# Masks of the diagonal operands in a held PSUM bank, and the last diagonal operand made ahead of the iteration

## Chip, cores, metric

One core of one Trainium2 chip. The metric is device time in microseconds (us), the median of several executions of one kernel; lower is better. Engines are named as the profile names them: PE = TensorE (PEld its weight loads), DVE = VectorE, ACT = ScalarE, POOL = GpSimd, SP = SyncE, which issues the DMAs here. L68 and L74 in the profile's lines are helpers through which nearly all instructions are issued, so the lines are told apart by the names of their tiles.

## The reference, cut to what matters

Nystrom attention over 8 batches, 8 heads, 576 positions of 64, then a layer norm and a two-layer MLP with a residual:

```python
A = sm(q, k_lm); Bm = sm(q_lm, k_lm); C = sm(q_lm, k)       # 32 landmarks
Z = Bm.T / (norms of Bm)
for _ in range(6):
    Z = 2 * Z - Z @ Bm @ Z
x = A @ Z @ C @ v
out = x + relu(layernorm(x) @ w_ch1) @ w_ch2
```

## The kernel before

The six steps run on `st`, which holds 32 columns of an iterate and 64 columns that go with it. The heads of a unit lie below each other in the partitions, so a step multiplies with a block-diagonal operand `ebd`, which VectorE makes by multiplying `st`, repeated four times, with a mask. `bmbd` is the same thing for `Bm` and is needed once, after the sixth step. Batch 0 does without `ebd`; batch 1 goes through `attention`, batches 2 to 7 (the third to eighth) through `attention2`, in groups (2), (3, 4), (5, 6), (7). The MLP's products (`psh`, `pso`) are issued between the attention's, as filler.

```python
    maskw = const.tile([P, 4, 4], FP16, name="maskw")
    mask16 = const.tile([P, 4], FP16, name="mask16")           # both in SBUF
    ...
    ps1 = ctx.enter_context(tc.tile_pool(name="ps1", bufs=1, space=bass.MemoryType.PSUM))
    ...
    def diagonal(name, src, W, mask):
        t = asm.tile([P, W, 4, LM], FP16, name=name, tag=name, bufs=1)
        dve.tensor_tensor(out=t[:], in0=src[:, :, None, :].broadcast_to([P, W, 4, LM]),
                          in1=mask, op=ALU.mult)
        return t

    def masks(W):
        return mask16[:, None, :, None].broadcast_to([P, W, 4, LM])
    ...
    # attention2, after the products pscv = C @ v
        dve.reciprocal(out=rcv_, in_=pcv[:, :, :, D])
        dve.tensor_tensor(out=rcv[:], in0=rcv[:], in1=cinv[:], op=ALU.mult)
    ...
        for it in range(6):
            psn = p1([P, W, LM + D], "psn")                    # p1: the one buffer of ps1
            for w in range(W):
                MM(psn[:, w, lo:], ebd[:, w, :, :]..., st[:, w, lo:])
            ...                                                # st = 2 st - psn, VectorE
            if it < 5:
                ebd = diagonal("ebd", st[:, :, 0:LM], W, masks(W))
            else:
                bmbd = diagonal("bmbd", bm16, W, maskw[:, 0:W, :, None].broadcast_to(...))
```

Meanwhile GpSimd prepares later batches: it casts q, k and v to fp16 (`nat`, `natv`), adds them up to landmarks (`asum`, `s`), and centres finished blocks for the MLP (`xn`). An `xn` is turned by a transposing DMA into `xnT`, which the `psh` products read.

The softmax here doesn't subtract the row's maximum and nothing guards it: scores larger than these inputs give would overflow.

Of the kernel before, what the change touches and what calls it, by code (L numbers as in the profile page):

```python
# [9 lines left out]
FP16 = mybir.dt.float16  # L10
FP32 = mybir.dt.float32
# [5 lines left out]
P = 128  # L17
# [3 lines left out]
def kernel(  # L21
# [10 lines left out]
    nc = tc.nc  # L32
# [6 lines left out]
    LM = 32  # L39
# [12 lines left out]
        name=nc.get_next_instruction_name(), act_func_set_id=6, ins=[], outs=[]))  # L52

    const = ctx.enter_context(tc.tile_pool(name="const", bufs=1))
# [15 lines left out]
    dve, pool, scalar = Ordered(nc.vector), Ordered(nc.gpsimd), Ordered(nc.scalar)  # L70
    act = scalar.activation

    def MM(o, l, r, rb=0, cb=0, start=True, stop=True, skip=False):
        keep(nc.tensor.matmul(o, l, r, start=start, stop=stop, tile_position=(rb, cb),  # L74
                              skip_group_check=(skip or cb != 0)))
# [78 lines left out]
    mask4 = const.tile([P, 4], FP32, name="mask4")  # L154
# [16 lines left out]


    maskw = const.tile([P, 4, 4], FP16, name="maskw")
    mask16 = const.tile([P, 4], FP16, name="mask16")
    nc.gpsimd.tensor_copy(out=mask16[:], in_=mask4[:])
    for w in range(4):
        nc.gpsimd.tensor_copy(out=maskw[:, w, :], in_=(mask4t if w % 2 else mask4)[:])

# [99 lines left out]
    mout = ctx.enter_context(tc.tile_pool(name="mout", bufs=4))  # L278

    ps1 = ctx.enter_context(tc.tile_pool(name="ps1", bufs=1, space=bass.MemoryType.PSUM))  # L280
    ps2 = ctx.enter_context(tc.tile_pool(name="ps2", bufs=2, space=bass.MemoryType.PSUM))
    psM = ctx.enter_context(tc.tile_pool(name="psM", bufs=3, space=bass.MemoryType.PSUM))


    def warm(n, cols):
# [5 lines left out]
# [4 lines that stand above are left out]
        return t  # L295

    def masks(W):
        return mask16[:, None, :, None].broadcast_to([P, W, 4, LM])


    def attention(bs):
        units = [(b, u) for b in bs for u in range(U)]
        W = len(units)
        first = bs[0] == 0
        pool1, tag1 = (psM, "pm") if first else (ps1, "p1")

        def p1(shape, name):
            return pool1.tile(shape, FP32, name=name, tag=tag1)

        def p2(shape, dtype, name):  # L310
            return ps2.tile(shape, dtype, name=name, tag="p2")

        pss = p1([P, 2, W, 64], "pss")
        xT = {}
        for w, (b, u) in enumerate(units):
# [35 lines left out]
            out=qbd[:],  # L351
            in0=pss[:, 0, :, :].rearrange("p u (e l) -> p (u e) l", e=2)[:, :, None, :]
# [5 lines left out]


        psb = p1([P, W, LM], "psb")  # L360
        for w in range(W):
            for h in range(4):
# [8 lines left out]
        bm16 = asm.tile([P, W, LM], FP16, name="bm16", tag="bm16")  # L371
# [8 lines left out]
        for w in range(W):  # L380
# [8 lines left out]
            if w % 2 == 1:  # L389
                yield  # L390

        psse_ = p1([P, 4, W * LM], "psse")
        psse = psse_[:, 0:2, :].rearrange("p a (u l) -> p a u l", u=W)
        MM(psse[:, 0, :, :], bones[:].rearrange("p a c -> p (a c)"), bm16[:])
        for w in range(W):
            for h in range(4):
# [1 line left out]
                MM(psse[sl, 1, w, :], bmT[sl, w, :], bmT[sl, w, :], rb=32 * h, cb=32 * h)  # L398
        dve.tensor_reduce(out=psse_[:, 2, 0:W], in_=psse[:, 0, :, :], axis=AX.X,
                                op=ALU.max)  # L400
        dve.tensor_scalar(out=psse_[:, 3, 0:W], in0=psse_[:, 2, 0:W], scalar1=1e-6,
                                scalar2=None, op0=ALU.add)
        cinv = asm.tile([P, W], FP32, name="cinv", tag="cinv")
        dve.reciprocal(out=cinv[:], in_=psse_[:, 3, 0:W])
        st = asm.tile([P, W, LM + D], FP16, name="st", tag="st")
        dve.tensor_tensor(out=st[:, :, 0:LM], in0=psse[:, 1, :, :],
                                in1=cinv[:, :, None].broadcast_to([P, W, LM]),
# [1 line left out]
        if not first:  # L409
            ebd = diagonal("ebd", st[:, :, 0:LM], W, masks(W))  # L410
# [23 lines left out]
        for it in range(6):  # L434
# [16 lines left out]
            if not first and it < 5:  # L451
                ebd = diagonal("ebd", st[:, :, 0:LM], W, masks(W))
            if it < W:
                w = it
# [17 lines left out]
        for w, (b, u) in enumerate(units):  # L472
            z = zcbd_buf[w]
            dve.scalar_tensor_tensor(
                out=z[:, :, 0:D],
                in0=pszc[:, w, None, :].broadcast_to([P, 4, D]), scalar=cinv[:, w:w + 1],
# [127 lines left out]
    def scores(pair, lm, xT, of, sc, name):  # L604
        tiles = {w: ps2.tile([P, NJ, 2 * LM], FP32, name="ps" + name, tag="p2") for w in pair}
        for (j0, j1) in ((0, 8), (8, NJ)):
            for x in range(2):
                for w in pair:
                    for h in range(4):
                        rows = ds(32 * h, 32)  # L610
                        cb = 32 * ((h + 2 * (w % 2)) % 4)
                        MM(tiles[w][ds(cb, 32), j0:j1, :], lm[rows, w, :, x],
                           xT[of, w][rows, j0:j1, :, :, x], rb=32 * h, cb=cb,
                           start=(x == 0), stop=(x == 1), skip=True)
        res = []
        for w in pair:
            t = aexp.tile([P, NJ * 2 * LM], FP16, name=name, tag="e")
            act(t[:], tiles[w][:].rearrange("p c t -> p (c t)"), AF.Exp, scale=sc)
            res.append(t)
        return res  # L620

    def attention2(bs, c):
        units, lm, xT = c.units, c.lm, c.xT
        W = len(units)

        def p1(shape, name):
            return ps1.tile(shape, FP32, name=name, tag="p1")


        psb = p1([P, W, LM], "psb")  # L630
        ecT = {}
        for y in range(W // 2):
# [7 lines left out]
            if y == W // 2 - 1:  # L640
# [5 lines left out]
                bm16 = asm.tile([P, W, LM], FP16, name="bm16", tag="bm16")  # L646
# [9 lines left out]
                ecT[w] = t  # L656
            yield

        psse_ = p1([P, 4, W * LM], "psse")
        psse = psse_[:, 0:2, :].rearrange("p a (u l) -> p a u l", u=W)  # L660
        MM(psse[:, 0, :, :], bones[:].rearrange("p a c -> p (a c)"), bm16[:])
        for w in range(W):
            for h in range(4):
# [1 line left out]
                MM(psse[sl, 1, w, :], bmT[sl, w, :], bmT[sl, w, :], rb=32 * h, cb=32 * h)  # L665
        dve.tensor_reduce(out=psse_[:, 2, 0:W], in_=psse[:, 0, :, :], axis=AX.X,
                                op=ALU.max)
        dve.tensor_scalar(out=psse_[:, 3, 0:W], in0=psse_[:, 2, 0:W], scalar1=1e-6,
                                scalar2=None, op0=ALU.add)
        cinv = asm.tile([P, W], FP32, name="cinv", tag="cinv")  # L670
        dve.reciprocal(out=cinv[:], in_=psse_[:, 3, 0:W])
        st = asm.tile([P, W, LM + D], FP16, name="st", tag="st")
        dve.tensor_tensor(out=st[:, :, 0:LM], in0=psse[:, 1, :, :],
                                in1=cinv[:, :, None].broadcast_to([P, W, LM]),
                                op=ALU.mult)
        ebd = diagonal("ebd", st[:, :, 0:LM], W, masks(W))


        pscv = ps2.tile([P, 2, 512], FP32, name="pscv", tag="p2")
        for y in range(W // 2):  # L680
            for j in range(SEG):
                if j == NJ:
                    yield
                for x in range(2):
                    w = 2 * y + x
# [8 lines left out]
            if y + 1 < W // 2:  # L694
                yield
        v_used.update(c.bs)
        pcv = pscv[:, :, 0:(W // 2) * (D + 1)].rearrange("p x (y e) -> p y x e", e=D + 1)
        rcv = asm.tile([P, W], FP32, name="rcv", tag="rcv")
        rcv_ = rcv[:].rearrange("p (y x) -> p y x", x=2)
# [3 lines left out]
            out=st[:, :, LM:LM + D].rearrange("p (y x) e -> p y x e", x=2),  # L703
            in0=pcv[:, :, :, 0:D],
# [4 lines left out]
        for it in range(6):  # L709
            lo = 0 if it < 5 else LM  # L710
            psn = p1([P, W, LM + D], "psn")
            for w in range(W):
                MM(psn[:, w, lo:], ebd[:, w, :, :].rearrange("p a l -> p (a l)"), st[:, w, lo:])
            stn = asm.tile([P, W, LM + D], FP16, name="st", tag="st")
            dve.scalar_tensor_tensor(out=stn[:, :, lo:], in0=st[:, :, lo:], scalar=2.0,
                                           in1=psn[:, :, lo:], op0=ALU.mult,
                                           op1=ALU.subtract)
            st = stn
            if it < 5:
                ebd = diagonal("ebd", st[:, :, 0:LM], W, masks(W))  # L720
            else:
                bmbd = diagonal("bmbd", bm16, W,
                                maskw[:, 0:W, :, None].broadcast_to([P, W, 4, LM]))
            if it < W // 2:
                for e in scores((2 * it, 2 * it + 1), lm["k"], xT, "q", sc_A, "ea"):
                    ea.append(e)
            yield
# [5 lines left out]
        for w in range(W):  # L733
            z = zcbd_buf[2 + w]
            dve.tensor_tensor(
                out=z[:, :, 0:D],
                in0=pszc[:, w % 2, None, ds(D * (w // 2), D)].broadcast_to([P, 4, D]),
# [241 lines left out]


    a0, a1 = attention((0,)), attention((1,))

    def run(*who):
# [97 lines left out]
    for c, after, count in zip(sets, sets[1:] + [None], counts):  # L1081
        for step, _ in enumerate(attention2(c.bs, c)):
            work(count[step])
            if late and step >= 3:
                late.pop(0)()
            if after and after.done < len(after.parts) and not (
                    after.k_by_pool and after.spread(step)):
                next_cast()
            if after and step >= (5 if after.k_by_pool else 1):
                after.next_job()  # L1090
        while after and (after.jobs or after.lms):
            work(8)
            next_cast()
            after.next_job()
# [34 lines left out]
```

## Time and profile before

| | before |
|---|---|
| median of the first 3 runs | 328.93 us (327.85 to 329.19) |
| profiled run | 328.16 us, span 326.4 us |
| busy PE / DVE / ACT / POOL | 96 / 54 / 47 / 47% |

A busy share averages over stages with different limits. In this kernel TensorE, VectorE and GpSimd are busy in the first 140 us (131.6, 104.6 and 120.4 us of them), and in the rest TensorE alone is busy without a pause (182.2 of 186.4 us; VectorE 70.2, GpSimd 33.2). The prediction shows the lines.

Three lines from the timelines of the kernel before that the result will be held against: a cast of GpSimd near 49 us, an `xn` at 137.54 us, and the first MLP product behind the last wait for `xnT` (start us, duration us, engine, line, operation, tiles, shape, and in brackets the idle time before it).

```profile
49.49 1.15 POOL L68 CAST nat<-stg 128x1152 f16<-128x1152 f32 x1 [0.27 <-DVE ebd L68]
...
137.54 0.69 POOL L68 TENSOR_SCALAR xn<-xblk,mvg 128x512 f16<-128x512 f32 x1
...
140.54 1.89 PE L74 MATMUL psh<-xnT,w 128*128 128x512 f16 x8 [0.39 <-DMA xnT<-xn]
```

From the first of them to the end of the `xn` at 137.54 us GpSimd has no pause of over 0.1 us. These are 88.74 us (138.24 - 49.49, with unrounded times). The transposing DMA that the `psh` waits for was issued at 136.85 us, before that `xn` began, so it reads an earlier one. SyncE had issued it and the two transposes ahead of it with no pause of over 0.1 us from 132.98 us on, just after an `xn` that ended at 132.96 us. From 140.54 us to the end are 185.9 us in which TensorE does not pause until the last store.

### The profile page before, as it was taken

The page shows a single profiled execution, that of the slowest core. Times are in us where ns is not written, and L with a number is a line of the kernel's source. Part 1 is how long each engine was busy: PE and PEld are TensorE (multiplying, and loading weights), DVE is VectorE, ACT ScalarE, POOL GpSimd, SP SyncE. Part 2 cuts the span into 40 slices and gives each one's busy share as a digit, 9 for nine tenths or more (in the row PEclk, how much of TensorE's full clock was granted, in tenths as well). Part 3 has the DMA queues.
Part 4 walks back from the last instruction along what each step waited for, and adds up shares of the span by engine and source line. Part 5 has one row for each costly group of instructions (what it writes and reads, how often), then busy time and mean ns, then how long its engine had stood idle before and what let it go on. Part 6 is the DMA issues. An engine that isn't in the chain of part 4 may idle for free.

```text
span 326.4 us, 8246 instructions
## 1 busy us (share of the span) xinstructions
PE 313.8 (96%) x3406; PEld 162.0 (50%) x3406; DVE 174.8 (54%) x396; ACT 153.3 (47%) x308; POOL 153.6 (47%) x242
## 2 busy tenths in 40 slices
PE   8889989998999999999999999999999999999995
PEld 7537864553445444535544445454444444444444
DVE  3568769879965588864147668722566110010012
ACT  3646662848960572967204672454046107305600
POOL 3489888999999999999800044200013000000000
PEclk9999999999999999999999999999999999999998
DMA  7999999998699854598035013510251126032023
GB/s 278 391 355 363 382 401 297 330 324 254 215 220 234 242 150 139 142 246 152 2 80 87 2 27 69 98 34 2 64 128 2 32 64 98 0 73 60 0 47 81
DMA packets 36685, 50.34 MB, mean 154 GB/s; under 512 B 17828, under 2 KB 22696, under 8 KB 36648
## 3 DMA queue, kind: packets, MB, share of 16 engines
q1 hardware_dynamic: 36488, 49.69, 54.6%
q8 instruction: 26, 0.43, 0.6%
q10 hardware_dynamic: 160, 0.13, 0.2%
q14 instruction: 11, 0.09, 0.1%
HBM read 36.70 MB, written 9.44 MB: 141 GB/s over the span
## 4 chain that ended last, share of the span: by engine, by line
PE 59%; POOL 24%; DMA 8%; issue 3%; DVE 2%; ACT 1%; SPq 1%; POOLq 0%
PE psh L74 28%; PE pso L74 26%; POOL asum L68 13%; POOL nat L68 6%; DMA w1stg<-in_moe_w_ch_dram 4%; DMA stg<-in_v_dram 3%; POOL natv L68 2%; POOL xn L68 2%; PE psy L74 1%; PE pscv L74 1%; POOL s L68 1%; SPq L90 1%; DMA xnT<-xn 1%; ACT xn L68 1%; DVE ebd L68 1%
## 5 line engine op out<-in xcount | busy, mean ns | idle before, releaser
L74 PE MATMUL psh<-xnT,w 128*128 128x512 f16 (+1 forms) x640 | 134.0, 358 | 0.8 <-issue 0.5
L74 PE MATMUL pso<-w,hT 128*128 128x512 f16 (+1 forms) x592 | 132.9, 374 | 0.0
L68 ACT ACTIVATE hT<-psh 128x512 f16<-128x512 f32 x144 | 85.0, 597 | 97.3 <-PE psh L74 97.0
L74 PEld LDWEIGHTS <-w 128*128 128x128 f16 x640 | 59.5, 98 | 56.5 <-issue 3.4
L74 PEld LDWEIGHTS <-hT 128*128 128x128 f16 x592 | 56.0, 98 | 57.3 <-issue 0.8
L68 DVE SCALAR_TENSOR_TENSOR ot<-pso,rstd,xblk 128x512 f32<-128x512 f32 (+1 forms) x37 | 27.1, 733 | 78.1 <-PE pso L74 78.0
L68 POOL CAST nat<-stg 128x1152 f16<-128x1152 f32 x28 | 32.6, 1173 | 3.7 <-DMA stg<-in_q_dram 1.5
L68 POOL TENSOR_TENSOR asum<-asum 128x256 f32<-128x256 f32 (+2 forms) x54 | 28.3, 524 | 4.2
L68 DVE TENSOR_TENSOR xblk<-psy,rcpd 128x512 f32<-128x512 f32 (+1 forms) x40 | 27.6, 691 | 1.8 <-DVE rcpd L68 0.2
L68 POOL TENSOR_TENSOR asum<-nat 128x576 f32<-128x576 f16 x18 | 24.1, 1338 | 1.5
L68 DVE SCALAR_TENSOR_TENSOR st<-st,psn 128x192 f16<-128x192 f16 (+3 forms) x36 | 14.3, 396 | 19.3 <-PE psn L74 19.2
L68 POOL TENSOR_SCALAR xn<-xblk,mvg 128x512 f16<-128x512 f32 x14 | 9.6, 694 | 30.7 <-ACT junk L68 30.7
L68 POOL TENSOR_SCALAR negm<-mvg 128x1 f32<-128x1 f32 x14 | 2.7, 191 | 45.0 <-DVE mvg L68 40.4
L68 POOL CAST natv<-stg 128x1152 f16<-128x1152 f32 (+2 forms) x17 | 17.9, 1077 | 9.1 <-DMA stg<-in_v_dram 9.1
L68 DVE TENSOR_TENSOR ebd<-st,mask 128x256 f16<-128x256 f16 (+1 forms) x30 | 21.2, 707 | 1.0
L68 DVE STREAM_TRANSPOSE xT<-nat 128x576 uint32<-128x576 uint32 x24 | 18.2, 759 | 0.8 <-POOL nat L68 0.8
L74 PE MATMUL psy<-zcbd,ea 128*128 128x260 f16 (+1 forms) x80 | 15.9, 276 | 0.4
L68 ACT ACTIVATE ea<-psea 128x576 f16<-128x576 f32 x12 | 7.2, 648 | 16.6 <-PE psea L74 16.6
L74 PE MATMUL idle<-zeros 128*128 128x128 f16 (+2 forms) x79 | 12.3, 295 | 1.1 <-DVE eps_ln L180 1.1
L74 PEld LDWEIGHTS <-ea 128*128 128x128 f16 (+1 forms) x80 | 7.3, 100 | 11.1 <-issue 3.4
L68 DVE BATCH_NORM_STATS2 st<-xblk 128x6 f32<-128x512 f32 x18 | 12.4, 689 | 0.5
L68 ACT ACTIVATE junk<-xblk 128x512 f16<-128x512 f32 x14 | 8.8, 625 | 8.0 <-DVE xblk L68 7.7
(115 smaller groups left out, 261.3 us busy)
## 6 DMA issues: line engine op xcount, KB each, us to landing
stg<-in_q_dram SPq DMA_DIRECT2D x16, 576.0 KB, 6.6
out_dram<-ot SPq DMA_DIRECT2D x70, 128.0 KB, 2.4
stg<-in_k_dram SPq DMA_DIRECT2D x15, 576.0 KB, 4.9
stg<-in_v_dram SPq DMA_DIRECT2D x9, 576.0 KB, 6.7
w1stg<-in_moe_w_ch_dram SPq DMA_DIRECT2D x16, 256.0 KB, 6.0
w2stg<-in_moe_w_ch_dram SPq DMA_DIRECT2D x16, 256.0 KB, 5.3
stg<-in_v_dram SPq DMA_DIRECT2D x14, 288.0 KB, 5.1
xnT<-xn SPq DMA_TRANSPOSE x28, 3.7
```

The costliest lines, as they stand in the source:

```text
L68: return lambda *args, **kw: keep(getattr(self.engine, op)(*args, **kw))
L74: keep(nc.tensor.matmul(o, l, r, start=start, stop=stop, tile_position=(rb, cb), skip_group_check=(skip or cb != 0)))
L90: keep(queue.dma_start(out=t[:, r, j, :], in_=rows[r][:, :, j, :].rearrange("r p j d -> p r j d")))
```

## The change

The intent: VectorE's product for a diagonal operand reads two tensors from SBUF, and in the kernel before such a product and GpSimd's work beside it are both slow (`ebd` up to 1487 ns in place of 692, GpSimd's first sum 1637 in place of 1275); with its mask in PSUM it reads only one. No PSUM buffer is added: the one of `ps1` becomes a bank that is held for good, with the masks in its last 16 columns and everything that used `ps1` in its first columns. `bmbd` is made ahead of the steps, where VectorE waited for `pscv` in three of four stages (2.9, 4.0 and 4.6 us in the kernel before). Cut to the core (the rest replaces `ps1.tile` by `bank_of`, and puts two scratch rows of `psse` into one, so that they fit below the masks):

```diff
-    mask16 = const.tile([P, 4], FP16, name="mask16")
-    nc.gpsimd.tensor_copy(out=mask16[:], in_=mask4[:])
+    bank = ps1.tile([P, 512], FP32, name="bank")
+    pmask = bank[:, 496:512].rearrange("p (w h) -> p w h", h=4)
+    nc.vector.tensor_copy(out=pmask, in_=maskw[:])
     def masks(W):
-        return mask16[:, None, :, None].broadcast_to([P, W, 4, LM])
+        return pmask[:, 0:1, :, None].broadcast_to([P, W, 4, LM])
 ...
         v_used.update(c.bs)
+        bmbd = diagonal("bmbd", bm16, W, pmask[:, 0:W, :, None].broadcast_to([P, W, 4, LM]))
         ...
             if it < 5:
                 ebd = diagonal("ebd", st[:, :, 0:LM], W, masks(W))
-            else:
-                bmbd = diagonal("bmbd", bm16, W,
-                                maskw[:, 0:W, :, None].broadcast_to([P, W, 4, LM]))
```

More of the change, by code (lines that the diff above doesn't have):

```diff
@@ L280, with bank_of @@
     ps1 = ctx.enter_context(tc.tile_pool(name="ps1", bufs=1, space=bass.MemoryType.PSUM))
+    bank = ps1.tile([P, 512], FP32, name="bank")
     ps2 = ctx.enter_context(tc.tile_pool(name="ps2", bufs=2, space=bass.MemoryType.PSUM))
     psM = ctx.enter_context(tc.tile_pool(name="psM", bufs=3, space=bass.MemoryType.PSUM))
+    pmask = bank[:, 496:512].rearrange("p (w h) -> p w h", h=4)
+    nc.vector.tensor_copy(out=pmask, in_=maskw[:])
+    def bank_of(shape, name):
+        n = 1
+        for d in shape[1:]:
+            n *= d
+        assert n <= 512 - 16
+        names = [f"a{i}" for i in range(len(shape) - 1)]
+        if len(names) == 1:
+            return bank[:, 0:n]
+        return bank[:, 0:n].rearrange(f"p ({' '.join(names)}) -> p {' '.join(names)}",
+                                      **{k: d for k, d in zip(names, shape[1:])})
     def warm(n, cols):
@@ L304, in attention @@
         first = bs[0] == 0
-        pool1, tag1 = (psM, "pm") if first else (ps1, "p1")
         def p1(shape, name):
-            return pool1.tile(shape, FP32, name=name, tag=tag1)
+            return psM.tile(shape, FP32, name=name, tag="pm") if first else bank_of(shape, name)
         def p2(shape, dtype, name):
@@ L390, in attention @@
                 yield
-        psse_ = p1([P, 4, W * LM], "psse")
+        psse_ = p1([P, 3, W * LM], "psse")
         psse = psse_[:, 0:2, :].rearrange("p a (u l) -> p a u l", u=W)
@@ L400, in attention @@
                                 op=ALU.max)
-        dve.tensor_scalar(out=psse_[:, 3, 0:W], in0=psse_[:, 2, 0:W], scalar1=1e-6,
+        dve.tensor_scalar(out=psse_[:, 2, W:2 * W], in0=psse_[:, 2, 0:W], scalar1=1e-6,
                                 scalar2=None, op0=ALU.add)
         cinv = asm.tile([P, W], FP32, name="cinv", tag="cinv")
-        dve.reciprocal(out=cinv[:], in_=psse_[:, 3, 0:W])
+        dve.reciprocal(out=cinv[:], in_=psse_[:, 2, W:2 * W])
         st = asm.tile([P, W, LM + D], FP16, name="st", tag="st")
@@ L624, in attention2 @@
         W = len(units)
-        def p1(shape, name):
-            return ps1.tile(shape, FP32, name=name, tag="p1")
+        p1 = bank_of
         psb = p1([P, W, LM], "psb")
@@ L657, in attention2 @@
             yield
-        psse_ = p1([P, 4, W * LM], "psse")
+        psse_ = p1([P, 3, W * LM], "psse")
         psse = psse_[:, 0:2, :].rearrange("p a (u l) -> p a u l", u=W)
@@ L667, in attention2 @@
                                 op=ALU.max)
-        dve.tensor_scalar(out=psse_[:, 3, 0:W], in0=psse_[:, 2, 0:W], scalar1=1e-6,
+        dve.tensor_scalar(out=psse_[:, 2, W:2 * W], in0=psse_[:, 2, 0:W], scalar1=1e-6,
                                 scalar2=None, op0=ALU.add)
         cinv = asm.tile([P, W], FP32, name="cinv", tag="cinv")
-        dve.reciprocal(out=cinv[:], in_=psse_[:, 3, 0:W])
+        dve.reciprocal(out=cinv[:], in_=psse_[:, 2, W:2 * W])
         st = asm.tile([P, W, LM + D], FP16, name="st", tag="st")
```

## The prediction

> **What bounds the kernel now.** I read the page first (busy shares, slices, chain), then the waits of TensorE, then its timeline around each wait, then the groups by form for VectorE and GpSimd in stretches with and without company.
>
> From the page, the busy shares and the slices:
>
> ```profile
> PE 313.8 (96%) x3406; PEld 162.0 (50%) x3406; DVE 174.8 (54%) x396; ACT 153.3 (47%) x308; POOL 153.6 (47%) x242
> PE   8889989998999999999999999999999999999995
> POOL 3489888999999999999800044200013000000000
> PE 59%; POOL 24%; DMA 8%; issue 3%; DVE 2%; ACT 1%; SPq 1%; POOLq 0%
> ```
>
> TensorE is busy 313.8 of 326.4 us, so all its idle time together is 12.6 us; no change to waits can give more. In the windows view it is idle nowhere from 160 us to the final store. What can be won lies before that. GpSimd is at 8 or 9 tenths up to slice 20 (163 us), and the chain puts 24% on it, between 49 and 137 us. So two engines run level until about 140 us; after that TensorE alone sets the end, and time won at 140 us reaches the end whole.
>
> TensorE's waits between 35 and 145 us:
>
> ```profile
> engine line waited for: us in total, times, longest us
> PE psn L74 <- DVE ebd L68: 2.1, 3, 0.9
> PE psh L74 <- issue: 0.5, 1, 0.5
> PE psn L74 <- DVE st L68: 0.4, 1, 0.4
> PE psh L74 <- DMA xnT<-xn: 0.4, 1, 0.4
> PE psec L74 <- DVE xblk L68: 0.4, 1, 0.4
> PE pscv L74 <- DVE ecT L68: 0.2, 1, 0.2
> ```
>
> Half of what is left to win there is one thing: the product of an iteration step waiting for ebd, the block-diagonal operand that VectorE makes from st and a mask. Why is ebd late? Groups by form, first from 160 to 240 us, where GpSimd is nearly idle, then the whole run; last TensorE's and VectorE's timelines at the worst place:
>
> ```profile
> L68 DVE TENSOR_TENSOR ebd<-st,mask 128x512 f16<-128x512 f16 x5 | 3.5, 692 | 0.2
> L68 DVE TENSOR_TENSOR ebd<-st,mask 128x256 f16<-128x256 f16 x6 | 2.5, 425 | 0.2
> ...
> L68 DVE TENSOR_TENSOR ebd<-st,mask 128x256 f16<-128x256 f16 x18 | 11.2, 624 | 0.6
> L68 DVE TENSOR_TENSOR ebd<-st,mask 128x512 f16<-128x512 f16 x12 | 10.0, 832 | 0.4
> ...
> 121.53 1.49 DVE L68 TENSOR_TENSOR ebd<-st,mask 128x512 f16<-128x512 f16 x1
> 123.07 0.29 PE L74 MATMUL psn<-st,ebd 128*128 128x64 f16 x4 [0.67 <-DVE ebd L68]
> ```
>
> The same operation takes 425 or 692 ns alone, but up to 1487 ns while GpSimd reads. GpSimd suffers too: its first sum of a tile, by form, from 141 to 153 us (no ebd there) and from 110 to 125 us (an ebd about every 2.5 us):
>
> ```profile
> L68 POOL TENSOR_TENSOR asum<-nat 128x576 f32<-128x576 f16 x3 | 3.8, 1275 | 0.2
> ...
> L68 POOL TENSOR_TENSOR asum<-nat 128x576 f32<-128x576 f16 x3 | 4.9, 1637 | 0.2
> ```
>
> [...]
>
> [...]
>
> [...] with one PSUM input the 256-element products zcbd take 411 ns, and the 512-element xblk<-psy,rcpd takes 691 ns. So I use 420 and 690 ns for the new ebd.
>
> [...] The mask now shares the bank of psn, psb and psse. The iteration is a strict ring (psn, st, ebd, next psn), so TensorE never writes the bank while ebd reads it; nothing in this trace tests it.
>
> **The change part by part.**
>
> 1. Order. TensorE has the same 3406 products in the same order, GpSimd one tiny mask copy fewer, VectorE one 16-element copy more at the start, ScalarE and the queues the same. The waits of psn on TensorE's own semaphore go, and no psn gains an other-engine wait that its ring did not have. The fixed bank thus costs nothing and by itself saves nothing I can see.
>
> 2. ebd with one SBUF input. VectorE: 30 ebd take 11.2 + 10.0 = 21.2 us; at quiet speed 18 x 0.424 + 12 x 0.692 = 15.9 us. So 5.3 us of VectorE time go, all before 124 us. On the path, gap by gap from TensorE's timeline:
>  - 41.8 us, 0.40 idle: the first ebd took 0.85, 0.42 over its floor, and delayed st behind it. Closed: 0.40.
>  - 48.1 us, 0.53 idle: ebd took 1.14, 0.72 over. Closed: 0.53. At 49.6 us, 0.10 idle behind an ebd of 0.70: closed.
>  - 77.6 us, 0.87 idle: the ebd in front took 1.08 (0.66 over), and the one before 1.05, which pushed back the 1.34 us reduction between them. Together 1.28 over: closed, 0.87.
>  - 123.1 us, 0.67 idle: ebd took 1.49, 0.80 over. Closed: 0.67.
>  Sum 2.57 us, call it 2.6.
>
> 3. GpSimd, which must come along or the gain turns into a wait for xnT. Over the run, groups against their quiet means: asum<-nat 24.1 - 18 x 1.275 = 1.15; asum of 256, 13.5 - 18 x 0.724 = 0.47; asum of 128, 8.9 - 18 x 0.455 = 0.71; casts to nat 32.6 - 28 x 1.142 = 0.62; and 0.56 of idle before two casts, put down to ebd. Together 3.5 us, nearly all before 137 us; I count 3.3. GpSimd has no idle time over 0.1 us from 49.5 to 137 us, so it moves forward by that. Its end is what releases xn, the transposing DMA and then the psh at 140.54 us (0.39 idle). If TensorE gains 2.6 and GpSimd 3.3, that gap closes too: up to 0.4 more.
>
> 4. bmbd ahead of the six steps. Before, bmbd (0.63 to 0.68 us) lies between the last st and pszc. But TensorE has filler there and shows no idle before pszc: it is worth nothing. At its new place, ahead of the reciprocal of pscv, VectorE waits for pscv in three of four stages (idle 12.1 us for four of those reciprocals over the run). At 69.7 us it does not, and 0.42 us more there pass psn's margin (70.49 to 70.88 us) by perhaps 0.1 us: -0.1.
>
> Sum: 2.6 + 0.3 - 0.1, less about 0.1 for new small waits = 2.7 us. From 328.93: 326.2 us, 0.8% faster.
>
> **Rivals.**
>
> A. GpSimd becomes the bound. If its slow stretches come from other things than ebd (VectorE's transposes run beside it too), it gains 1 us, and TensorE then waits for xnT at 140 us. For: the chain has GpSimd without a break from 60 to 137 us. Against: from 141 to 153 us there are none of these iterations and its forms are at their floors. It would make 327.9 us.
>
> B. The PSUM operand is slower than I take it[...]. [...]
>
> C. TensorE is throughput-bound even where it seems to wait: the gaps close, and the following products, now queued more densely, do not start earlier, or a new wait (xblk, a score's exponent on ScalarE) takes their place. Against: the timelines show fillers of 1.7 us that end before psn, so TensorE really runs dry. Would give 327.5 us.
>
> D. More than the named gaps: with 5.3 us off VectorE in its fullest stretch (8 tenths busy from 40 to 100 us), other waits (ecT 0.2, xblk 0.4) shrink. Limit: all idle of TensorE from 35 to 145 us, about 5 us; 325.3 us likely the most.
>
> **Range and chances.** The three times of before spread over 1.3 us, so a median carries some 0.5 us. B and small forms of C and A are more likely than D: 325.2 to 327.5 us. Over 2% would need 6.6 us, more than TensorE's idle time after the first 35 us: 0.02. Slower by 2% needs a collision or a wait that the order does not show: 0.01.
>
> **What would show each step.** ebd rows near 420 and 690 ns in every stretch, with or without GpSimd beside them (step 2[...]). TensorE's wait for ebd at or near zero. asum<-nat near 1275 ns between 110 and 125 us (step 3). The psh now at 140.54 us starting 2.5 to 3 us earlier, with the same length from there to the end. If TensorE's idle before that psh grows to over 1 us, rival A holds. If bmbd's move shows a new wait of psn near 70 us of over 0.3 us, step 4 is wrong. A time over 328 us would mean that the gaps were not on the path at all.

The sum came to 2.7 us: 2.6 for TensorE's gaps, 0.3 for the gap before `psh`, less 0.1 for `bmbd` and 0.1 for new waits. Cut, where marked, is what no trace of this case had shown: the reason given for why an `ebd` with one SBUF input keeps its quiet speed beside GpSimd, so that step 2 rests there on an assumption of mine; an argument that VectorE loses no speed by it; a sentence on two engines in one bank; and the figure of rival B with the gain worked out from it, so that B stands only as a doubt. The 420 and 690 ns rest on `zcbd` (411 ns) and `xblk` (691 ns), products with one PSUM input in the kernel before.

## The result

| | before | changed |
|---|---|---|
| median, 6 runs each | 329.06 us (327.85 to 331.2) | 325.48 us (324.74 to 325.64) |
| ratio, with 95% interval | | 0.9879 (0.9845 to 0.9912) |
| ratio on another chip, 11 and 5 runs | | 0.9894 (0.9876 to 0.9912) |
| profiled span | 326.4 us | 323.4 us |

A ratio is the mean time of one kernel's fast runs over that of the other's of the same rounds, so it is not quite the ratio of the medians. The gain is 1.1 to 1.2%, some 3.5 to 4 us, where I had said 2.7. The two profiled runs differ by 3.05 us (328.16 and 325.11).

The page of the changed kernel: busy shares, the slices of TensorE and GpSimd, and the chain.

```profile
PE 313.4 (97%) x3406; PEld 163.8 (51%) x3406; DVE 170.7 (53%) x397; ACT 152.7 (47%) x308; POOL 149.7 (46%) x241
PE   8889999899999999999999999999999999999995
POOL 3389879999999999999500044200023000000000
PE 61%; POOL 23%; issue 3%; ACT 1%; DMA 1%; DVE 1%; POOLq 0%
```

TensorE is as busy as before, VectorE has 4.1 us less, GpSimd 3.9 us less. GpSimd has not left the chain: it holds 23% of a shorter span.

The groups by form of the changed kernel (busy us, mean ns), `ebd` over the whole run, and GpSimd's first sum from 110 to 125 us:

```profile
L68 DVE TENSOR_TENSOR ebd<-st,bank 128x512 f16<-128x512 f16 x12 | 8.2, 687 | 0.4
L68 DVE TENSOR_TENSOR ebd<-st,bank 128x256 f16<-128x256 f16 x18 | 7.6, 420 | 0.6
...
L68 POOL TENSOR_TENSOR asum<-nat 128x576 f32<-128x576 f16 x4 | 5.1, 1280 | 0.3
```

Every `ebd` is at its quiet speed, 420 and 687 ns in the mean and 689 at most, with GpSimd beside it or not, and GpSimd's sum went from 1637 to 1280 ns.

TensorE's waits in the changed kernel from 35 to 145 us (`bank` stands for `psn` and all else that lies in the held bank):

```profile
engine line waited for: us in total, times, longest us
PE psec L74 <- DVE xblk L68: 0.8, 2, 0.4
PE psh L74 <- DMA xnT<-xn: 0.8, 1, 0.8
PE bank L74 <- DVE st L68: 0.5, 1, 0.5
PE bank L74 <- DVE qbd L68: 0.2, 1, 0.2
```

The wait for `ebd` is gone. The wait for `xnT`, which I expected to close, is twice as long: TensorE comes to it first, and what it waits for comes from GpSimd. The lines of the changed kernel's timelines that answer to the three of before:

```profile
49.75 1.15 POOL L68 CAST nat<-stg 128x1152 f16<-128x1152 f32 x1 [0.28 <-PE bank L74]
...
134.52 0.70 POOL L68 TENSOR_SCALAR xn<-xblk,mvg 128x512 f16<-128x512 f32 x1
...
137.48 1.89 PE L74 MATMUL psh<-xnT,w 128*128 128x512 f16 x8 [0.76 <-DMA xnT<-xn]
```

GpSimd starts its stretch 0.26 us later and ends it 3.02 us earlier: 85.47 us in place of 88.74. The `psh` starts 3.06 us earlier, and from there to the end are 185.9 us again.

Both kernels issue the same 3406 products in the same order, so they can be compared one by one. TensorE's lead over the kernel before was 1.29 us at 49.6 us (the gaps of batch 1 had closed), but **0.13 us** at 70.9 us: it had given the lead back, 0.55 us of it before `psec`, 0.64 us before the first step of batch 2. From there to 123 us it grew to 3.42 us, and the wait for `xnT` cut it to 3.06. So there were two hypotheses to tell apart: TensorE's own gaps add up to the gain (my prediction), or **theory G**: GpSimd's stretch sets the time, and what TensorE wins beyond it is waited away.

### The profile page after: what moved, and what is told of

Read it like the earlier page. It is cut to its first block, busy times and chain, and to the rows that moved or that the text cites. A ratio compares the mean times of both kernels' runs of the same rounds, so it can differ in the third digit from the quotient of the medians.

```text
span 323.4 us, 8246 instructions
## 1 busy us (share of the span) xinstructions
PE 313.4 (97%) x3406; PEld 163.8 (51%) x3406; DVE 170.7 (53%) x397; ACT 152.7 (47%) x308; POOL 149.7 (46%) x241
## 4 chain that ended last, share of the span: by engine, by line
PE 61%; POOL 23%; issue 3%; ACT 1%; DMA 1%; DVE 1%; POOLq 0%
PE psh L74 29%; PE pso L74 26%; POOL asum L68 12%; POOL nat L68 6%; POOL natv L68 2%; POOL xn L68 2%; PE pscv L74 1%; PE psy L74 1%; POOL s L68 1%; PE bank L74 1%; DMA xnT<-xn 1%; ACT xn L68 1%; PE psea L74 1%; PE psec L74 1%; ACT xT L68 0%
## 5 line engine op out<-in xcount | busy, mean ns | idle before, releaser
L68 POOL CAST nat<-stg 128x1152 f16<-128x1152 f32 x28 | 31.8, 1144 | 3.7 <-DMA stg<-in_k_dram 1.7
L68 POOL TENSOR_TENSOR asum<-asum 128x256 f32<-128x256 f32 (+2 forms) x54 | 27.0, 500 | 4.2
L68 POOL TENSOR_TENSOR asum<-nat 128x576 f32<-128x576 f16 x18 | 23.0, 1276 | 1.5
L68 DVE SCALAR_TENSOR_TENSOR st<-st,bank 128x192 f16<-128x192 f16 (+3 forms) x30 | 12.2, 408 | 15.8 <-PE bank L74 15.7
L68 DVE TENSOR_TENSOR ebd<-st,bank 128x256 f16<-128x256 f16 (+1 forms) x30 | 15.8, 527 | 1.0
L74 PE MATMUL idle<-zeros 128*128 128x128 f16 (+2 forms) x79 | 13.2, 318 | 1.1 <-DVE eps_ln L178 1.1
```

The source lines that it names most:

```text
L68: return lambda *args, **kw: keep(getattr(self.engine, op)(*args, **kw))
L74: keep(nc.tensor.matmul(o, l, r, start=start, stop=stop, tile_position=(rb, cb), skip_group_check=(skip or cb != 0)))
```

## Experiments

Sixteen runs, three of them repeats of an earlier kernel. All gave correct results, those with constants in a bank that TensorE also writes included; by the program's order TensorE does not write there while `ebd` reads, and what an overlap would do was not tested. "To before" is the ratio to the kernel before on the same chip.

**1. A control.** The kernel before once more.

> The kernel before, unchanged, as a control and as a second look at it. The profiled run of before took 328.16 us, but its six runs have a mean of 329.3 and go from 327.9 to 331.2, while the six of the change go from 324.7 to 325.6. Theory S (scatter): where VectorE and GpSimd collide differs from run to run, so before scatters by its nature; then the copy against before gives a ratio near 1.000, but its runs spread over 1.5 us or more again, and its profile shows other ebd durations over 1 us at other places than the first profile (there 1.14, 1.05, 1.08, 1.06, 1.49 us). Rival: the scatter was of that chip or session; then the copy's ten runs stay within 1 us and the collisions are where they were.

Measured: 0.9996 (0.9975 to 1.0016), its runs from 328.10 to 329.77 us. After 110 us the collisions were elsewhere: `ebd` of over 1 us at 112.4 and 117.9 us (1.59 and 1.52), where the first profile had 0.84 and 0.69, and none at 121.5 us. Before 101 us they lay where they had been, one at 74 us a little under 1 us now. So where two instructions meet differs by run in part. The sum differs less: GpSimd's stretch was 89.01 us. The scatter of 1.67 us is as the theory had it, but kernels with masks in PSUM scatter by 0.7 to 1.8 us too (below), so most of it has another source.

**2. The parts one by one.** Masks back in SBUF, with the rest of the change:

```diff
-        return pmask[:, 0:1, :, None].broadcast_to([P, W, 4, LM])
+        return maskw[:, 0:1, :, None].broadcast_to([P, W, 4, LM])
     (and bmbd's mask from maskw)
```

> The change with its masks read from SBUF again (held bank and early bmbd stay). Theory [...]: all of the gain is the mask's place, so this is as slow as before: ratio to before 0.997 to 1.003, ebd of 256 elements back to a mean near 620 ns with single ones over 1 us, TensorE's wait for ebd back near 2 us. Rival 1 (early bmbd is worth something) or rival 2 (the held bank saves waits): ratio 0.990 to 0.995.

Measured: 1.002 (1.0002 to 1.0038), `ebd` of 256 elements at a mean of 636 ns. The gain is gone.

`bmbd` late, masks in PSUM (`bmbd` moved back behind the sixth step):

> The change with bmbd in its old place, after the sixth step, masks in PSUM. Theory: the move of bmbd is worth nothing or costs 0.1 us, so the ratio to before is that of the whole change, 0.985 to 0.991, and the 0.48 us wait of psn for st near 70.7 us that the changed kernel shows is gone. Rival 1: the move carries 0.3% or more; ratio 0.991 or higher.

Measured: 0.9914 (0.9894 to 0.9934). Most of the gain without the early `bmbd`. The 0.48 us wait before the first step was there as well (at 72.0 us), so it does not come from `bmbd`'s move.

The held bank alone (masks in SBUF, `bmbd` late):

> The kernel before with the held bank alone: masks in SBUF, bmbd late. Theory: the bank's fixed place changes only which semaphore a product waits on, ratio 0.998 to 1.002. Rival 2 (TensorE's waits on its own semaphore, which the held bank removes, cost time at each of the 24 steps): ratio 0.993 to 0.997.

Measured: 1.000 (0.9982 to 1.0017). The bank by itself is worth nothing.

**3. Which batches carry it.** The change whole, again, with the next three on one chip:

> The changed kernel once more, on the chip of the next three. Known now: in every kernel so far the psh behind the last wait for xnT (140.54 us before, 137.48 us changed) starts 185.9 us before the end, and from the third cast to nat (49.5 to 51 us) to the end of the last xn of that group GpSimd takes 88.6 to 89.0 us with masks in SBUF and 85.5 us with masks in PSUM. Theory G (GpSimd sets the pace from there): this profile shows 85.5 us again, and the ratio to before is 0.987 to 0.990. What is over 3.3 us must then lie in when the third cast starts. Rival (TensorE's own waits for ebd are the gain, as I predicted): ratio near 0.992, for these were 2.6 us.

Measured: 0.9894 (0.9876 to 0.9912), median 325.22 us; stretch 85.43 us; `psh` to end 185.9 us.

> The change with bmbd in its old place, again, now beside the whole change. Theory G: GpSimd's stretch is 85.5 us with either place of bmbd, so the two differ by under 0.3 us. Rival (the early bmbd is worth the 0.6 us that lay between the two kernels' medians of different sessions): 0.5 to 0.8 us slower than the whole change, with a wait before pszc in the profile.

Measured: 0.9915 (0.9895 to 0.9934), median 325.85 us, 0.6 us slower than the whole change, as before. The stretch is 85.45 us, the same. So not theory G's "under 0.3 us"; more under 7.

Masks in PSUM for batch 1 alone, or for batches 2 to 7 alone:

```diff
 a1_psum: attention2's ebd and bmbd
-                ebd = diagonal("ebd", st[:, :, 0:LM], W, masks(W))
+                ebd = diagonal("ebd", st[:, :, 0:LM], W, masks_sbuf(W))
 a2_psum: the same in attention
```

> The change with masks in PSUM in the stage of the second batch alone (its six ebd from 40 to 49 us); batches 3 to 8 read theirs from SBUF. My predicted sum (TensorE's gaps add up): 0.40 + 0.53 + 0.10 = 1.0 us faster than before, ratio 0.997. Theory G: TensorE's lead at 50 us is given back by 71 us to waits that hang on GpSimd, so only what moves the third cast counts: 0 to 0.5 us faster, ratio 0.9985 to 1.001; GpSimd's stretch stays near 88.8 us.

Measured: **1.0012** (0.9994 to 1.0031).

> The complement: masks in PSUM for batches 3 to 8, in SBUF for the second batch's stage. My predicted sum: 0.87 + 0.67 + 0.3 = 1.8 us faster than before, ratio 0.9945. Theory G: GpSimd's stretch 85.5 us, so 3.3 us faster, ratio 0.9895 to 0.9905, whatever TensorE waits for at 48 us.

Measured: **0.9906** (0.9890 to 0.9922).

These two decide against my sum. TensorE's waits (same stretch of time as above), first of a1_psum, then of a2_psum, and a2_psum's timeline around the `psh`:

```profile
PE bank L74 <- DVE ebd L68: 1.9, 3, 0.9
PE psh L74 <- DMA xnT<-xn: 0.9, 1, 0.9
...
PE bank L74 <- DVE st L68: 0.7, 2, 0.4
PE bank L74 <- DVE ebd L68: 0.6, 1, 0.6
...
137.72 0.38 PE L74 MATMUL pso<-w,hT 128*128 128x512 f16 x1
137.93 1.24 PE L74 MATMUL psh<-xnT,w 128*128 128x512 f16 x5
```

In a1_psum the three gaps of batch 1 that I had counted as 1.03 us are closed, and the kernel is no faster. In a2_psum they are all open (0.43, 0.56 and 0.11 us at 42 to 50 us in its trace), and it has nearly the whole gain. The stretch is 88.97 us in a1_psum and 85.44 us in a2_psum. But a2_psum is no plain case of theory G: its list has no wait for `xnT`, and the last transposing DMA landed at 137.04 us, 0.9 us before the `psh`. There TensorE came last, and its own lead, 2.61 us at the `psh`, is the gain of the profile.

**4. The collision without the late `ebd`.** `bmbd_late`, with one more product behind each `ebd` of batches 2 to 7, which nobody reads:

```diff
                 ebd = diagonal("ebd", st[:, :, 0:LM], W, masks(W))
+                diagonal("bmbd", st[:, :, 0:LM], W, maskw[:, 0:1, :, None]...)   # dup_sbuf; pmask in dup_psum
```

> bmbd_late (masks in PSUM, ratio to before 0.9915) with one more product of the same size behind each ebd of batches 3 to 8, whose result nobody reads (it goes to bmbd's buffer, which is rewritten before its use), its mask in SBUF. ebd itself is on time. Theory G: [...] GpSimd's stretch goes from 85.5 back to 88 to 89.5 us and the ratio to before is 0.999 to 1.005, though ebd stays at 420 and 690 ns. Rival (a late ebd is the cost): ratio 0.991 to 0.994, the price of VectorE's extra work alone.

Measured: 1.0019 (1.0001 to 1.0036), stretch 88.46 us.

> Control for dup_sbuf: the same extra product, its mask in PSUM. Theory G: GpSimd's stretch stays at 85.5 us; VectorE has some 7 us more to do before 125 us, so a few waits of TensorE grow; ratio to before 0.991 to 0.996, at least 1.5 us faster than dup_sbuf. Rival: no difference between the two.

Measured: 0.9991 (0.9975 to 1.0007), stretch 87.20 us, of which GpSimd idled 1.73 us before two `xn`, behind ScalarE. **My expectation failed.** The extra VectorE work alone costs 2.5 us (0.9991 against 0.9915 for bmbd_late). That it pushes back the step's own `st`, so that TensorE comes later and GpSimd waits for TensorE's rows, is my reading; of it, only GpSimd's idle time is shown. The pair differs by 0.3% and not by the 0.5% or more that I had asked for. In both profiles TensorE comes to the `psh` (141.80 and 140.53 us) without a wait. So against bmbd_late the added work costs 2.5 us with its mask in PSUM and 3.4 us with its mask in SBUF. The pair does not tell which of the two the kernel before suffered from.

**5. The last two-SBUF-input operation.** In the changed kernel, `rcv<-rcv,cinv` has 4 or 2 elements and takes 161 ns where GpSimd is idle. VectorE's and GpSimd's timelines in the (3, 4) stage:

```profile
106.91 0.82 DVE L68 TENSOR_TENSOR rcv<-rcv,cinv 128x4 f32<-128x4 f32 x1
...
106.44 1.27 POOL L68 TENSOR_TENSOR asum<-nat 128x576 f32<-128x576 f16 x1
```

It ends at 107.73 us, 0.02 us after GpSimd's sum does (107.71 us). The product of 2 elements at 69.43 us took 0.94 us and ended at 70.37 us, a sum of GpSimd beside it at 70.34 us.

```diff
-        dve.reciprocal(out=rcv_, in_=pcv[:, :, :, D])
-        dve.tensor_tensor(out=rcv[:], in0=rcv[:], in1=cinv[:], op=ALU.mult)
+        inv = bank[:, 480:480 + W]
+        dve.reciprocal(out=inv.rearrange("p (y x) -> p y x", x=2), in_=pcv[:, :, :, D])
+        dve.tensor_tensor(out=rcv[:], in0=inv, in1=cinv[:], op=ALU.mult)
```

> The change, with its last two-SBUF-input VectorE operation mended too: rcv<-rcv,cinv of 4 or 2 elements takes 161 ns alone but 0.82 to 0.98 us in the two stages where GpSimd runs, and ends with the GpSimd instruction it waited for. The reciprocal now goes to four free columns of the held bank. rcv<-bank,cinv should take 160 to 230 ns everywhere, and the 0.48 us wait of TensorE for st near 71 us go. Theory G: GpSimd sets the time, so the gain over the whole change is 0 to 0.3 us (ratio to before 0.9885 to 0.9900). Rival (TensorE's wait adds up): 0.5 us or more, 0.9878.

Measured: 0.9891 (0.9875 to 0.9907). The tile's view, then TensorE's wait for `xnT`:

```profile
L68 DVE TENSOR_TENSOR rcv<-bank,cinv x4: 159/160/161, 69.6 to 216.1; 128x2 f32<-128x2 f32 x2, 128x4 f32<-128x4 f32 x2
...
PE psh L74 <- DMA xnT<-xn: 1.3, 1, 1.3
```

It took 160 ns everywhere, the 0.48 us wait at 71 us went, and the time stayed within the noise: the 0.5 us turned up again as a longer wait for `xnT` (1.33 us in place of 0.76). Stretch 85.49 us. This is theory G in small: a TensorE wait was removed, and in the profile nothing of it reached the end.

**6. GpSimd's time itself, longer and shorter.**

> The change, with two of the four casts of v for batches 4 and 5 made twice by GpSimd (2 x 1.15 = 2.3 us more, near 85 us; the same values are written). No other engine has more to do. Theory G: GpSimd's stretch 87.8 us and the time 2.3 us more less nothing, for GpSimd is already the last to come (TensorE waits 0.7 us for xnT): 327.5 us, ratio to before 0.996 to 0.998, TensorE's wait for xnT near 3 us. Rival (GpSimd's time only moves along): ratio unchanged at 0.989 to 0.990.

```diff
+                if self.bs == (3, 4) and w >= 2:
+                    pool.tensor_copy(out=natv_of[b][:, ds(SEG * u, SEG), 0:D], in_=stg[:])
                 pool.tensor_copy(out=natv_of[b][:, ds(SEG * u, SEG), 0:D], in_=stg[:])
```

Measured: **0.9983** (0.9970 to 0.9995), median 328.02 us. No other engine got work. The stretch is 88.06 us, 2.6 us longer than in the two profiles of the change, and the profiled time (327.94 us) is 2.2 to 2.8 us longer than theirs (325.76 and 325.11). TensorE's waits in it:

```profile
PE psy L74 <- DVE xblk L68: 1.3, 2, 1.1
PE psh L74 <- DMA xnT<-xn: 1.3, 1, 1.3
```

The wait for `xnT` is 1.3 us and not 3, but there is a new one of 1.3 us some 9 us before it, in the rows. So more time on GpSimd moves the end of the changed kernel back, about one for one.

For the other direction, casts of v go to ScalarE:

```diff
+                if self.bs == (3, 4) and w % 2 == 1:      # v_act_rcv; gp_minus1: w == 3; gp_minus2: also (5, 6), w == 0
+                    scalar.copy(natv_of[b][:, ds(SEG * u, SEG), 0:D], stg[:])
+                    return
```

> rcv_psum, and two of the four casts of v for batches 4 and 5 (1.15 us each on GpSimd, near 84 to 88 us) are given to ScalarE. Theory G: GpSimd's stretch falls to about 83.2 us, and the time falls until TensorE's own work is the bound: it waits 0.7 us for xnT now, plus the 0.5 us that rcv frees, so 0.7 to 1.3 us faster than the whole change, ratio to before 0.985 to 0.987. Rival (GpSimd is not the bound): no gain, or a loss of some tenths through ScalarE's longer queue.

> rcv_psum (ratio 0.9891, TensorE waits 1.3 us for xnT) with one cast of v for batch 5 on ScalarE, the one that had its data in v_act_rcv. Theory G: GpSimd's stretch 84.3 us, gain 0.8 to 1.15 us, ratio to before 0.9855 to 0.987, TensorE's wait for xnT down to 0.2 to 0.5 us. Rival: ratio stays 0.989.

> gp_minus1 and one cast of v for batch 6 on ScalarE, in its idle time near 121 to 126 us. GpSimd's stretch 83.2 us. Theory G with TensorE close behind: TensorE's wait for xnT goes and its own work becomes the bound, so 1.2 to 1.6 us faster than rcv_psum, ratio 0.984 to 0.986; not the whole 2.3 us. Rival: 0.989.

Measured: 1.0067 (1.0048 to 1.0086), 1.0119 (1.0099 to 1.0140) and 1.0131 (1.0113 to 1.0148). All three failed as tests, for one reason, seen in gp_minus1's ScalarE and TensorE timelines:

```profile
80.57 1.15 ACT L68 CAST natv<-stg 128x1152 f16<-128x1152 f32 x1 [5.37 <-DMA stg<-in_v_dram]
...
82.27 2.29 PE L74 MATMUL psh<-xnT,w 128*128 128x512 f16 x5 [5.91 <-ACT hT L68]
```

ScalarE reaches the cast before its load has landed and idles 5.37 us, and a product of TensorE waits 5.91 us for an `hT` that ScalarE makes after the cast. GpSimd comes to its casts of v later: in the changed kernel it makes these four from 83.76 us on and does not wait for a load there. In v_act_rcv the other cast stood in front and had taken the stall (4.45 us), which is why I thought that this one had its data. Whether less work on GpSimd would make the kernel faster stays untested.

**7. Does early `bmbd` work through `rcv`?** rcv_psum with `bmbd` late:

> rcv_psum with bmbd in its old place. If the early bmbd works by moving rcv<-rcv,cinv to where GpSimd blocks it for less long (1.27 and 0.86 to 1.09 us with bmbd late, 0.93 and 0.82 to 0.98 us with it early), then with rcv out of GpSimd's way the place of bmbd no longer matters: within 0.3 us of rcv_psum, ratio 0.988 to 0.990. If bmbd's own 0.4 to 0.7 us between the last st and the next product is what it saves, late_rcv is 0.5 to 0.7 us slower than rcv_psum: 0.991.

Measured: 0.9907 (0.9894 to 0.9921). By the numbers that is the second answer, but the profile does not bear it out: stretch 85.51 us and wait for `xnT` 1.33 us, both as in rcv_psum (85.49 and 1.33). The two profiles differ by 0.9 us in when the stretch begins.

What the traces of the decisive kernels show, in order of the stretch. "Begins" is the start of the third cast to `nat` after 40 us, where the stretch begins; it ends with the same `xn`, counted by its place in GpSimd's order (my expectations call this `xn` the last of its group; it is the next one). "`psh`" is the same product in all, number 1849 of TensorE's 3406. TensorE waits for `xnT` before it, 0.2 to 1.3 us, in all rows but two: in bmbd_late_again the wait is 0.04 us, in a2_psum there is none.

| kernel | masks, batches 2 to 7 | `bmbd` | begins | stretch | `psh` | span | to before |
|---|---|---|---|---|---|---|---|
| mask_sbuf | SBUF | early | 50.83 | 89.04 | 142.00 | 327.9 | 1.0020 |
| before_copy | SBUF | late | 49.62 | 89.01 | 140.74 | 326.6 | 0.9996 |
| a1_psum | SBUF | early | 50.35 | 88.97 | 141.48 | 327.4 | 1.0012 |
| before | SBUF | late | 49.49 | 88.74 | 140.54 | 326.4 | 1 |
| bank_only | SBUF | late | 50.16 | 88.64 | 141.00 | 326.9 | 1.0000 |
| gp_plus | PSUM, 2 casts more | early | 49.80 | 88.06 | 140.34 | 326.2 | 0.9983 |
| late_rcv | PSUM | late | 50.55 | 85.51 | 138.60 | 324.5 | 0.9907 |
| rcv_psum | PSUM | early | 49.66 | 85.49 | 137.68 | 323.6 | 0.9891 |
| changed | PSUM | early | 49.75 | 85.47 | 137.48 | 323.4 | 0.9879 |
| bmbd_late | PSUM | late | 50.97 | 85.46 | 138.49 | 324.4 | 0.9914 |
| bmbd_late_again | PSUM | late | 50.44 | 85.45 | 138.36 | 324.2 | 0.9915 |
| a2_psum | PSUM | early | 49.75 | 85.44 | 137.93 | 323.8 | 0.9906 |
| after_again | PSUM | early | 50.53 | 85.43 | 138.18 | 324.0 | 0.9894 |

In every row span less `psh` is 185.9 us. Begin plus stretch gives the end of GpSimd's part; `psh` follows 2.1 to 2.8 us later. The begin scatters by 1.5 us and goes with a load: in the six profiles that begin at 50.3 us or later, GpSimd had just waited 0.7 to 1.1 us for weights (`w2stg`), and in the six that begin by 49.8 us it had not. The two pauses between the three casts are 0.26 to 0.30 us in all, whatever the trace names as their end. The stretch does not scatter: 88.6 to 89.0 with masks in SBUF, 85.4 to 85.5 with masks in PSUM.

None of these is a version that clearly beats the change; rcv_psum equals it.

## Why the prediction was wrong

**The cause** of the gain was named right. It is the place of the masks: back in SBUF the whole gain is lost (mask_sbuf, 1.002, `ebd` of 256 elements at a mean of 636 ns), in PSUM `ebd` is at its quiet speed (689 ns at most, 1487 before), and the held bank costs and saves nothing (bank_only 1.000). Rival B, a slow PSUM operand, fell: 420 and 687 ns against 425 and 692. Of rival C the first half fell: the products behind the closed gaps did start earlier. Its second half, a new wait in their place, came true for batch 1, and for `xblk`, which it had named. Rival D's 325.3 us is nearly the time measured, but by luck: of the waits that it named, the one for `ecT` stayed at 0.15 us and the one for `xblk` grew from 0.39 to 0.77 us.

**The step that failed is the sum of step 2, "Sum 2.57 us, call it 2.6", and the place that step 3 gave GpSimd**, as one that "must come along". I had GpSimd's term right, 3.3 us in the prediction and 3.3 us in the stretches (88.74 - 85.47), and then used it only to ask whether one small gap would close. But before the change GpSimd was the later of the two: TensorE waits 0.2 to 1.0 us for `xnT` in all five profiles with these masks in SBUF. So what TensorE wins alone is given back (a1_psum), and the gain could be as large as GpSimd's 3.3 us, as far as TensorE kept up.

The sum was also too small for what it meant to add. I took a gap's idle time for its delay. The record of an MLP product, which stands before most of these gaps, lasts 0.38 us, and the next one starts 0.22 us after its start where nothing is waited for (five `pso` took 1.24 us together in the kernel before), so that up to 0.16 us of a delay lies hidden under the record before. Compared product by product, the five gaps were worth 0.43, 0.70, 0.26, 1.03 and 0.84 us of TensorE's lead: 3.26 us and not 2.57.

Term by term: batch 1's gaps (0.40, 0.53, 0.10 of idle time) are worth nothing while GpSimd is slow (a1_psum, 1.0012). TensorE closed them and gave the lead back by 71 us, to new waits before `psec` and before the first step. With GpSimd fast they may be worth some of it: a2_psum leaves them open, begins its stretch with the changed kernel at 49.75 us and is as long in it, but its `psh` starts 0.45 us later, without a wait. The medians on one chip were 325.67 and 325.22 us; the intervals overlap. The 0.87 and 0.67 us of the later batches are part of a lead that grew by 3.3 us between 71 and 123 us: 1.03 and 0.84 of it are these gaps, 0.62 lies before a `psh` at 110.4 us, where the trace puts the wait down to nothing, and five steps of 0.18 to 0.29 us, less three small losses, are the rest. The 0.3 us for the gap before `psh` had the wrong sign; that wait grew from 0.39 to 0.76 us.

**The base** was a second error of the range. I subtracted from the median, 328.93, what I had counted in a run that took 328.16. The profile's begin of the stretch, 49.49 us, is the earliest of all kernels in the table; an average run probably begins later. In the profiled pair the whole difference is 3.05 us, and the ratio of the first session (0.9879) has one high run of before in it, 331.2 us; on another chip it was 0.9894, or 3.5 us. What between 3.1 and 4 us is the stretch and what is scatter of the begin cannot be told from profiles of one run each.

**Rival A** (GpSimd becomes the bound) came closest, but with the wrong sign for the time. I argued that GpSimd as the bound would make the gain smaller. It was the bound already, by the 0.2 to 1.0 us of waiting above, and it gained 3.3 us where I had given this rival 1 us.

**Step 4, `bmbd`.** I predicted a loss of 0.1 us. The sign that I had named for an error, a wait of over 0.3 us near 70 us, appeared (0.48 us), but `bmbd` does not make it: it is there with `bmbd` late, and it goes when `rcv`'s collision goes (rcv_psum). I had also read `bmbd` as taking 0.63 to 0.68 us before; in the last stage it took 0.42. Early `bmbd` was 0.6 us better by medians in the one pair on one chip (325.22 and 325.85 us), and 0.9891 against 0.9907 in a pair on two chips; the intervals overlap in both. With masks in SBUF it was the other way (1.002 early, 1.000 late). With masks in PSUM, the profiles with it late begin the stretch at 50.4 to 51.0 us and those with it early at 49.7 to 50.5, before the first `bmbd` is made, so no mechanism of `bmbd` that I can name reaches there. The collision of `rcv` is ruled out (late_rcv). This stays open.

**What is shown and what is not.** Shown: the masks of batches 2 to 7 carry the gain; their place shortens GpSimd's stretch by 3.1 to 3.6 us, whichever two profiles are compared; a GpSimd stretch longer by 2.6 us with nothing else changed costs 2.2 to 2.8 us. GpSimd's chain sets the end where TensorE waits for `xnT`, and in a2_psum TensorE's own does: both became shorter, by 3.3 and 2.6 us. Not shown: how much of the kernel before's time would have gone if only `ebd` were on time, since no run put the `ebd` of batches 2 to 7 on time with GpSimd's stretch as before and no work added; in dup_psum more work on VectorE also cost (2.5 us). And that less GpSimd work would gain more: three attempts stalled on loads.

## What to carry to other kernels

When two engines run level, work out for each the uninterrupted run that ends in the last wait between them, and take the gain from the one that comes last, before the change and after it; here three closed gaps of the other engine, 1.03 us of idle time, were worth nothing (a1_psum, 1.0012), and in the changed kernel TensorE's lead of 1.29 us after them shrank to 0.13 us before that wait. Measure a gap by how much later the next product starts, not by the idle time shown (here 3.26 us against 2.57). Look for VectorE instructions with two SBUF inputs wherever GpSimd is busy, however small they are: in the changed kernel a product of 2 elements took 935 ns in place of 161 and ended at 70.37 us, just after a GpSimd sum (70.34 us). (Here the cure of that one gained nothing: rcv_psum, 0.9891, against 0.9894 for after_again.) GpSimd, too, took 88.74 us before and 85.47 changed for the same work, with 12 `ebd` and 2 `bmbd` in that time. And subtract from the time of the run that was profiled, not from the median of others.
